# A new list of steps, up to the second batch, for an attention and gated-MLP kernel

## The chip, the cores and the metric

The kernel runs on one core of one Trainium2 chip. The metric is the device time of one execution in microseconds (us). The engines are TensorE (PE in the rows; PEld is its loading of weights), VectorE (DVE), ScalarE (ACT), GpSimd (POOL) and SyncE (SP), which issues the transfers (DMA).

## The reference

```python
def _attn_ref(q, k, v):            # 8 batches, 8 heads, 576 positions, head size 64
    scores = scale * np.matmul(q, k.transpose(0, 1, 3, 2))
    scores = np.where(mask, scores + bias[None], -1e9)   # 0 <= rel < 128; bias: -slope * |rel|
    scores = scores - np.max(scores, axis=-1, keepdims=True)
    attn = np.exp(scores)
    attn = attn / (np.sum(attn, axis=-1, keepdims=True) + 1e-09)
    return np.matmul(attn, v)

def _moe_ref(x, w_in, g_ln, w_sg, b_sg, w_out):          # x: attention out, 576 x 512 a batch
    h = gelu_tanh(x @ w_in)                              # 1024 wide
    u, v = h[..., :512], h[..., 512:]
    v_n = (v - mean(v)) / np.sqrt(var(v) + 1e-6) * g_ln
    v_s = np.einsum('ts,bsd->btd', w_sg, v_n) + b_sg[None, :, None]
    return x + (u * v_s) @ w_out
```

## The kernel before

The work is cut into 32 pairs of heads (four pairs to a batch) for the attention and into eight batches for the gated MLP. It is written as 2027 small steps, each a closure for one engine, with a name of a letter or two and numbers. The table of numbers is the string `ORDER`: the loop at the end takes the steps in that order, and each engine's instructions are tied into the order in which they are emitted. So an engine never goes past an instruction that waits, and the list alone decides what stands behind what. Buffers are handed out in list order too: a step that takes a buffer waits for the one that the list frees first.

The names that matter here, n being the pair (0 to 3 are batch 0, 4 to 7 batch 1):

- `q`n, `L`n: transfers of queries and keys, and of values. `i`k: transfer of one of 12 weight blocks (0 to 7 of w_in, 8 to 11 of w_out); `wl`c, `tl`, `bl`, `gb`: transfers of the spatial table w_sg, its bias and g_ln.
- `d`k (ScalarE, two instructions), `m`k, `b`k, `o`k (VectorE), `+`k (GpSimd), `H`k (ScalarE), `-`k (VectorE for odd k, GpSimd for even): a weight block is turned from 64 bits into a high and a low half. `wH`c, `w-`c: the same for w_sg.
- `a`n and `c`n (TensorE): scores; `*`n: both, from pair 5 on. `A B C G` (VectorE): bias and row minima of a quarter each; `e E f F j` (ScalarE): exponentials; `R` (VectorE): inverse sums; `s S r`: scaling (ScalarE or GpSimd); `t T z` (TensorE): transposes; `X Y` (VectorE): the masked halves that the product with the values needs; `P`, `p`: small copies on ScalarE for the first 64 rows; `V` (TensorE): product with the values; `x` (ScalarE) and `2`n (VectorE): its result to SBUF; `h` (ScalarE), `l` (GpSimd), `k`: its high and low halves, which the MLP multiplies.
- `w`tc and `v`bt (TensorE): the v half of the first MLP product, piece by piece for batch 0; `vg`: its gelu; `nv..`, `vn`: its norm; `u`bfi: the u half; `uc`: its copy out; `ug`: its gelu; `tt tj tg nt tn`: the same for the last 64 rows; `y`: the spatial product; `gm gh gl`: the gate; `O`, `oa`, `D`: the last product, its addition and its store.
- `W`i (TensorE): dummy products of a zero tile, 2 to 12 each, 51 in all, that compute nothing and need nothing but a PSUM bank. They are among the first steps in both lists.

A GpSimd step of the first stretch is one instruction; from the step `v33` on (`HALVED_FROM`) its large ones are cut in two. PSUM is three pools of two tiles (`ps_s`, `ps_a`, `ps_m`); v, u, y and O products take turns in `ps_m`. One ScalarE table holds the exponential, another the gelu, so a change from `e`-like steps to `vg`, `tg`, `ug` or back loads a table.

Of the kernel before, what the change touches and what calls it, by code (L numbers as in the profile page):

```python
# [21 lines left out]
def attention_gmlp(  # L22
# [1129 lines left out]
    ORDER = """
        q0 i2 d2 W8 W1 a0 c0 i1 A0 B0 m2 b2 o2 C0 e0 d1 E0 j0 f0 +2 G0 m1 F0 q1 a1 c1 b1 R0 A1 o1 B1 C1 wl2 i3 q3 i0
        L0 H2 wH2 W0 G1 s0 -2 S0 +1 w-2 t0 j1 d3 e1 r0 F1 E1 f1 X0 T0 W7 W2 W3 z0 W6 W11 P0 d0 Y0 m3 V0 b3 R1 o3 m0 b0
        o0 r1 z1 i5 wl3 p0 s1 +0 a3 A3 B3 W4 t1 W5 W10 c3 X1 C3 G3 wH3 d5 x0 e3 H0 f3 E3 20 S1 +3 w-3 -0 q2 L1 i6 i4
        L2 i7 h0 H1 F3 j3 P1 d6 T1 a2 Y1 A2 B2 l0 V1 R3 m5 s3 b5 -1 m6 o5 b6 o6 d4 x1 m4 21 +6 S3 t3 W9 X3 p1 r3 d7 h1
        j2 E2 e2 m7 c2 C2 G2 w00 z3 T3 w20 w30 f2 F2 P3 +5 l1 Y3 b7 R2 b4 o4 o7 s2 S2 +4 +7 L3 q5 V3 x3 23 i9 wl1 p3
        wH1 d9 r2 H5 q4 L4 i10 gb tl w10 t2 X2 T2 w11 z2 w01 Y2 H3 P2 h3 H7 V2 x2 p2 H4 l3 m9 b9 -3 -5 22 -7 w31 w21
        *5 A5 B5 h2 H6 e5 l2 w02 w32 v00 E5 vg00 v03 w12 v01 w22 v02 o9 C5 G5 nv00b nv00c -6 -4 +9 nv00p tH d10 k3 H9
        nv00h vg01 k2 -9 vn00 m10 b10 o10 vg03 f5 +10 u000 u001 nv30b nv30c nv10b nv30p H10 uc00 j5 nv30h F5 vn03 R5  # L1160
        nv10c -10 u030 a4 A4 u031 B4 vg02 k0 k1 e4 nv20b s5 r5 S5 nv10p w-1 t- nv20p t5 z5 c4 u020 X5 T5 C4 G4 Y5
        nv20c j4 uc03 E4 nv10h tt0 f4 P5 F4 nv20h i11 L5 q6 i8 bl q7 wl0 V5 u021 vn01 R4 vn02 tj0 d8 p5 x5 tg0 wH0 s4
        r4 S4 w-0 t4 25 X4 nt0b nt0p u010 z4 T4 u011 Y4 nt0c P4 uc02 d11 bH V4 nt0h p4 x4 uc01 ug0 b- tn0 m11 m8 24
        b11 o11 b8 y000 y001 *7 +11 gm00 A7 o8 +8 B7 C7 j7 e7 H11 -11 Us0 y020 y021 y030 G7 gm02 Us1 E7 H8 -8 gh00 f7
        h4 gh02 F7 Us2 *6 y010 Us3 R7 A6 B6 C6 s7 t7 S7 T7 y031 E6 gl02 r7 gl00 G6 X7 f6 e6 j6 F6 z7 y011 h5 L7 L6 q8
        q9 Y7 R6 gm03 gm01 P7 V7 gh03 gh01 p7 Uh0 s6 r6 S6 gl01 t6 T6 X6 x7 27 Y6 Oa0 gl03 z6 O00 P6 V6 Us4 oa00 h7
        Uh1 x6 p6 l7 l4 l5 26 Ul0 Ul1 O01 *8 A8 B8 C8 Us5 G8 h6 k5 f8 j8 e8 l6 u100 u101 k6 k7 E8 *9 Us6 F8 oa01 Us7
        A9 R8 B9 k4 Uh2 j9 uc10 u130 s8 r8 S8 u131 t8 u110 C9 uc13 E9 e9 f9 T8 tt1 X8 Ul2 G9 F9 R9 Y8 q10 Ud0 L9 D01
        Ud1 q11 L8 Ud2 D00 z8 u111 s9 r9 S9 tj1 Us8 uc11 P8 t9 V8 u120 tg1 x8 X9 28 Us9 nt1b T9 u121 Y9 nt1c O03 nt1p
        z9 Uh3 nt1h uc12 P9 Ul3 ks0 ks1 ks2 V9 p9 x9 p8 oa03 ks3 29 ks4 tn1 kh0 kh1 kl0 O02 ks5 *10 A10 B10 C10 G10  # L1170
        j10 e10 E10 f10 F10 oa02 kl1 v10 *11 v11 A11 R10 vg10 vg11 B11 nv01b nv01c C11 nv11b r10 s10 nv01p S10 nv11p
        z10 t10 ug1 v12 nv11c X10 v13 T10 P10 nv11h vn11 nv01h vn10 vg12 nv21b G11 vg13 nv31b Y10 nv21c nv31c ks6
        nv21p h9 l9 nv31p ya100 ya110 ya101 ya111 f11 e11 nv21h nv31h j11 kd0 q12 q13 L10 L11 D03 kd1 D02 V10 vn12 kh2
        F11 E11 vn13 y100 y101 y110 y111 ks7 kl2 gm10 ks8 ks9 R11 kh3 gm11 kl3 y120 y121 s11 t11 y130 gh11 gl11 y131
        x10 210 gm12 gt11 p10 h8 gh15 X11 gm13 O11 S11 gl15 r11 gt12 T11 z11 O15 h10 gh12 gh16 gh13 P11 Y11 oa11 gl12
        V11 x11 p11 gl16 gt13 O16 211 gh17 oa15 oa16 gt14 *13 gl13 O13 gl17 ut25 oa13 O17 A13 oa17 O12 B13 oa12 h11
        gh14 gl14 l8 O14 C13 oa14 G13 l10 l11 E13 k10 uh25 k9 k11 k8 v20 v21 vg20 ul25 vg21 j13 ut26 ut27 nv02b nv02c
        nv02p nv02h nv12b nv12p nv12c nv12h vn20 vn21 *12 tt2 U21 kd2 lu21 lu22 q14 lu20 L12 D11 D10 q15 L13 tj2 U25
        uh27 f13 uh26 e13 ue21 A12 B12 ut24 ul27 ul26 U26 F13 ue25 U23 uh24 E12 ue26 U27 C12 ue23 G12 R13 e12 f12 j12
        F12 U22 ue27 R12 ul24 U24 ue22 r12 s12 z12 t12 S12 tg2 nt2b nt2p s13 X12 nt2c ue24 v22 T12 Y12 v23 vg22 nv22b  # L1180
        P12 nt2h tn2 vg23 V12 p12 x12 nv32b nv32c 212 nv22c nv22p nv32p S13 h12 l12 r13 ug2 nv22h nv32h ya200 ya210
        *14 A14 B14 vn22 ya201 t13 ya211 z13 vn23 y200 y201 X13 gm20 C14 y210 y211 y220 T13 gm21 G14 E14 P13 f14 gh21
        j14 F14 e14 Y13 gl21 y221 *15 y230 R14 A15 gt21 B15 gm22 C15 r14 s14 S14 y231 gh25 f15 gm23 gl25 gt23 gt22 z14
        t14 V13 E15 gh23 P14 p13 x13 gh27 O21 gh22 j15 X14 213 lo21 q16 lo22 D13 q17 D12 lo20 L14 L15 T14 O25 G15 Y14
        gh26 V14 p14 F15 x14 e15 gl23 gl27 gl22 oa21 gl26 O26 oa25 O23 ut35 gt24 214 R15 oa26 oa23 *16 A16 B16 C16 O27
        s15 S15 r15 z15 t15 h14 k12 gh24 h13 E16 P15 j16 l13 gl24 l14 G16 oa27 X15 k13 e16 uh35 F16 f16 O22 T15 Y15
        O24 *17 R16 oa22 oa24 A17 B17 V15 s16 r16 S16 x15 p15 215 h15 ul35 l15 C17 f17 e17 t16 X16 T16 G17 ut37 Y16
        L16 q19 lu32 D21 lu30 D23 L17 q18 lu31 D20 v30 z16 k15 k14 j17 P16 F17 E17 tt3 tj3 *18 V16 R17 ut36 tg3 vg30
        nt3b nt3c nt3p uh37 x16 ul37 nt3h v31 216 nv03b tn3 U31 uh36 vg31 ue31 U35 A18 B18 nv13b ut34 ul36 U36 r17 s17
        t17 z17 ue35 uh34 ue36 C18 nv13c U33 ue33 X17 S17 nv03p nv13p ul34 U37 U32 ue37 T17 U34 nv13h P17 j18 E18 f18  # L1190
        vn31 ue32 G18 nv03c Y17 nv03h ue34 p16 F18 e18 vn30 v33 D22 R18 *19 vg33 V17 x17 ug3 A19 s18 B19 C19 nv33b 217
# [81 lines left out]
```

## Time and profile before

| | |
|---|---|
| median of 3 runs | 581.13 us (581.12 to 581.57) |
| the profiled execution | 581.97 us, of which the span of instructions is 580.3 us |
| TensorE, busy share of the span | 97% |
| VectorE | 82% |
| ScalarE | 66% |
| GpSimd | 53% |

Times in the rows count from the start of the span. A busy share is a mean over stretches that have different limits; matmuls overlap in the records, so a busy TensorE is one without pauses, not one at its peak. In a row, the bracket gives the idle time just before the instruction and what ended it; xN is the number of instructions that the row merges.

### The profile page before, as it was taken

To read this page: it belongs to the slowest core of one execution; us is meant where nothing else is said; L and a number is where in the kernel's file an instruction comes from. 1 tells how busy PE (TensorE), PEld (TensorE's weight loads), DVE (VectorE), ACT (ScalarE), POOL (GpSimd) and SP (SyncE) were. 2 spreads that over 40 slices of the span, in tenths; PEclk is the share of its full clock that TensorE was granted. 3 is DMA by queue.
4 is the path that set the end of the run, shared out by engine and by line. 5 is a ranking of instruction groups with operands and counts; after the bars stand their busy time and mean duration, and the time that the engine had idled before them with its cause. 6 is when DMAs were issued, how large, how long until landed. Compare 5 with 4: busy or idle time off the path is not lost.

```text
span 580.3 us, 14668 instructions
## 1 busy us (share of the span) xinstructions
...
## 2 busy tenths in 40 slices
...
GB/s 299 212 224 107 127 102 83 7 272 33 210 37 64 215 37 98 144 180 141 60 184 38 105 236 167 48 101 153 143 121 64 211 4 196 3 32 98 171 1 82
DMA packets 43562, 69.79 MB, mean 120 GB/s; under 512 B 3554, under 2 KB 31202, under 8 KB 43492
## 3 DMA queue, kind: packets, MB, share of 16 engines
...
HBM read 56.27 MB, written 12.58 MB: 119 GB/s over the span
## 4 chain that ended last, share of the span: by engine, by line
PE 86%; DVE 4%; DMA 3%; ACT 3%; POOL 2%; issue 1%; SPq 0%; DVEq 0%; POOLq 0%
PE ps_m L1061 13%; PE ps_m L609 12%; PE ps_m L907 12%; PE ps_m L611 11%; PE ps_m L610 11%; PE ps_a L350 4%; PE ps_a L281 4%; PE ps_s L387 3%; PE ps_m L387 3%; PE ps_s L281 3%; DMA wst<-w_sgT 2%; DMA qk<-qkT 1%; PE ps_m L943 1%; PE ps_m L942 1%; DVE e L298 1%
## 5 line engine op out<-in xcount | busy, mean ns | idle before, releaser
L337 POOL TENSOR_TENSOR e<-e,rr 128x256 f32<-128x256 f32 (+2 forms) x116 | 80.3, 715 | 95.1 <-DVE rr L326 90.5
L314 ACT ACTIVATE e<-e,stats 128x128 f32<-128x128 f32 (+1 forms) x288 | 110.6, 386 | 19.4 <-DVE stats L298 18.9
L227 POOL TENSOR_TENSOR region<-u,region 128x288 fp32r<-128x288 f32 (+1 forms) x78 | 77.6, 1014 | 44.8 <-ACT region L1008 16.2
L359 DVE TENSOR_TENSOR px<-ps_a,m_both 128x1024 f32<-128x1024 f32 x64 | 77.4, 1215 | 6.2 <-PE ps_a L350 4.9
L609 PE MATMUL ps_m<-ws,region 128*128 128x288 f32 x256 | 78.3, 306 | 0.0
L611 PE MATMUL ps_m<-ws,region 128*128 128x288 f32 x256 | 75.7, 296 | 0.0
L610 PE MATMUL ps_m<-ws,region 128*128 128x288 f32 x256 | 75.6, 295 | 0.0
L732 POOL TENSOR_TENSOR rs<-rs,mhalf 128x1 f32<-128x1 f32 (+1 forms) x40 | 30.6, 766 | 58.3 <-DVE rs L729 54.6
L221 POOL TENSOR_TENSOR xs<-xf,xs 128x288 fp32r<-128x288 f32 (+1 forms) x48 | 51.1, 1086 | 14.5 <-ACT xs L404 14.5
L314 ACT ACTIVATION_READ_ACCUMULATOR e<-e,stats 128x1 f32 x288 | 54.3, 189 | 0.0
L1008 ACT ACTIVATE region<-u 128x576 fp32r<-128x576 f32 x35 | 23.6, 684 | 43.4 <-PE ps_m L610 17.4
L609 PEld LDWEIGHTS ps_m<-ws,region 128*128 128x128 f32 x256 | 48.3, 189 | 1.5 <-issue 1.1
L610 PEld LDWEIGHTS ps_m<-ws,region 128*128 128x128 f32 x256 | 48.2, 188 | 0.1
L611 PEld LDWEIGHTS ps_m<-ws,region 128*128 128x128 f32 x256 | 48.1, 188 | 0.1
L609 PE MATMUL ps_m<-wi,xs 128*128 128x512 f32 x112 | 46.7, 417 | 0.9 <-ACT vg L788 0.9
L1068 DVE TENSOR_TENSOR xf<-ps_m,xf 128x576 f32<-128x576 f32 x48 | 35.7, 750 | 10.9 <-PE ps_m L1061 10.1
L611 PE MATMUL ps_m<-wi,xs 128*128 128x512 f32 x112 | 44.3, 395 | 0.0
L610 PE MATMUL ps_m<-wi,xs 128*128 128x512 f32 x112 | 44.2, 395 | 0.0
L948 DVE TENSOR_TENSOR u<-ps_m,u 128x576 f32<-128x576 f32 x32 | 24.0, 750 | 19.7 <-PE ps_m L943 12.6
L350 PE MATMUL ps_a<-ident,e 128*128 128x128 f32 x256 | 38.0, 276 | 0.2
L298 DVE CUSTOM_DVE_ANT_0 e<-ps_s,bias 128x128 f32<-128x128 f32 (+1 forms) x140 | 34.9, 286 | 2.6
L1061 PE MATMUL ps_m<-region,sum 128*128 128x288 f32 x252 | 36.5, 298 | 0.0
(213 smaller groups left out, 1606.2 us busy)
## 6 DMA issues: line engine op xcount, KB each, us to landing
...
```

Source lines behind the costliest of these rows:

```text
L221: (engine or nc.gpsimd).tensor_tensor(out[:, cs], a[:, cs], b[:, cs], op)
L227: nc.gpsimd.tensor_tensor(out[:, fs], a[:, fs], b[:, fs], ALU.subtract)
L298: nc.vector.tensor_tensor_reduce(out=dst, in0=src, in1=bs, scale=-1.0 / math.sqrt(D), scalar=3e38, op0=ALU.add, op1=ALU.min, accum_out=acc)
L314: nc.scalar.activation(x, x, AF.Exp, bias=self.nm[0:n, i:i + 1], scale=-1.0, accum_out=self.sm[0:n, i:i + 1])
L337: nc.gpsimd.tensor_tensor(x[:, z:z + step, :], y[:, z:z + step, :], self.rr[0:n, i + z:i + z + min(k, step)].rearrange("p (m o) -> p m o", ...
L350: burst([lambda t=t: nc.tensor.transpose(cv[:, t // 2, t % 2], self.pr[j][:, t, :].rearrange("p (h c) -> p h c", h=2), ident[:, j * R:j * ...
L359: nc.vector.tensor_tensor(xv, cv, mv, ALU.mult)
L609: nc.tensor.matmul(dst, ah, bh, start=(first and i == 0), stop=False)
L610: nc.tensor.matmul(dst, ah, bl, start=False, stop=False)
L611: nc.tensor.matmul(dst, al, bh, start=False, stop=(last and i == n - 1))
L907: nc.tensor.matmul(dst, left(n, g, c)[:, ms], right(n, h, c), start=first and c == 0 and k == 0, stop=c == 1 and k == 2, skip_group_check= ...
L1061: nc.tensor.matmul(dst, p, q, start=first and f == 0 and k == 0, stop=f == 1 and k == 2, skip_group_check=True)
```

## The change

The list is a new one from its start to the step `V10` (631 steps, some 162 us into the execution); what follows is as before. The same steps are in it, with the same instructions and sizes; only their order differs, and with it which buffer of a pool a step gets. Among the moves: fourteen dummy products instead of eight ahead of the first scores, the weight blocks in the order 2, 0, 1, 4, 3 instead of 2, 1, 3, 0, 5, the tables w_sg 2 and 3 much later, and the scores of pair 4 ahead of most u products.

```diff
-        q0 i2 d2 W8 W1 a0 c0 i1 A0 B0 m2 b2 o2 C0 e0 d1 E0 j0 f0 +2 G0 m1 F0 q1 a1 c1 b1 R0 A1 o1 B1 C1 wl2 i3 q3 i0
...
+        q0 i2 q1 W3 W2 W4 W10 a0 c0 W9 W1 W5 a1 A0 B0 d2 C0 m2 G0 b2 o2 A1 i0 +2 e0 E0 f0 F0 j0 d0 B1 R0 j1 s0 m0 b0
...
```

The first place is ScalarE up to the copy P0 (`p_0`), which pair 0's product V0 needs. `e` and `stats` with 126 are pair 0's, with 128 pair 1's; L193 and L195 are a d step, L314 exponentials, L332 scalings. From pair 1's first exponentials (j1 before, E1 now) on, before:

```order
L314 ACTIVATE e_1_124,stats_128<-e_1_124,stats_128 128x64
L193 ACTIVATE wst<-wst 128x512
L195 ACTIVATE tmp<-wst 128x512
L314 ACTIVATE e,stats_128<-e,stats_128 128x128 x2
L332 ACTIVATE e_0_122<-e_0_122,rr 128x64
L314 ACTIVATE e,stats_128<-e,stats_128 128x128 x6
L366 COPY p_0_119<-ps_a 128x128
L193 ACTIVATE wst<-wst 128x512
L195 ACTIVATE tmp<-wst 128x512
```

and now:

```order
L314 ACTIVATE e,stats_128<-e,stats_128 128x128 x2
L193 ACTIVATE wst<-wst 128x512
L195 ACTIVATE tmp<-wst 128x512
L314 ACTIVATE e,stats_128<-e,stats_128 128x128 x6
L193 ACTIVATE wst<-wst 128x512
L195 ACTIVATE tmp<-wst 128x512
L332 ACTIVATE e_1_124<-e_1_124,rr 128x64
L332 ACTIVATE e_0_122<-e_0_122,rr 128x64
L332 ACTIVATE e<-e,rr 128x128 x4
L193 ACTIVATE wst<-wst 128x512
L195 ACTIVATE tmp<-wst 128x512
L366 COPY p_0_119<-ps_a 128x128
```

Before, the copy stood behind the weights 2, 1 and 3; now the weights 0, 1, 4 and 3 (beside 2) and the scaling of pair 1 stand ahead of it.

The second place is VectorE ahead of the two masked halves of pair 2 (L359, X2 and Y2), from the inverse sums R2 (L325, L326) on; L399 is the step 23. Before:

```order
L325 TENSOR_SCALAR rr<-stats_130 128x9
L326 RECIPROCAL rr<-rr 128x9
L199 TENSOR_SCALAR tmp<-tmp 128x512
L201 SCALAR_TENSOR_TENSOR tmp<-wst,tmp 128x512 x2
L399 TENSOR_TENSOR xf_134<-ps_s,xf_134 128x512
L359 TENSOR_TENSOR px<-ps_a,m_both 128x4x256 x2
L197 TENSOR_SCALAR tmp<-tmp 128x512
L199 TENSOR_SCALAR tmp<-tmp 128x512
```

and now:

```order
L325 TENSOR_SCALAR rr<-stats_130 128x9
L326 RECIPROCAL rr<-rr 128x9
L197 TENSOR_SCALAR tmp<-tmp 128x512
L211 TENSOR_TENSOR wi<-tmp,wi 128x512
L199 TENSOR_SCALAR tmp<-tmp 128x512
L201 SCALAR_TENSOR_TENSOR tmp<-wst,tmp 128x512
L399 TENSOR_TENSOR xf_134<-ps_s,xf_134 128x512
L359 TENSOR_TENSOR px<-ps_a,m_both 128x4x256 x2
```

Before, b4, o4 and o7 (L199, L201) stood between, and m9 and b9 behind X2 and Y2; now m9, the subtraction -1 (L211), b9 and o9 stand ahead of them.

The third place is ScalarE's first gelus of v (L788) with the table loads, the exponentials of pairs 5 and 4 (L314), the norms' high halves (L740) and the copy uc00 (L842). Before:

```order
L788 ACTIVATE vg<-ps_m 128x512
L410 CAST xs<-xs 128x64
L788 ACTIVATE vg<-ps_m 128x512
L314 ACT_TABLE_LOAD
L314 ACTIVATE e,stats_130<-e,stats_130 128x128 x2
L206 ACTIVATE wo<-tmp 128x512
L842 COPY u<-ps_m 128x576
L314 ACTIVATE e_1_124,stats_130<-e_1_124,stats_130 128x64
L740 ACTIVATE region<-vg,rs 128x4x128
L314 ACTIVATE e,stats_130<-e,stats_130 128x128 x2
L1239 ACT_TABLE_LOAD
L1239 ACTIVATE warm<-mhalf 128x1
```

and now:

```order
L1239 ACT_TABLE_LOAD
L1239 ACTIVATE warm<-mhalf 128x1
L788 ACTIVATE vg<-ps_m 128x512 x2
L314 ACT_TABLE_LOAD
L314 ACTIVATE e,stats_130<-e,stats_130 128x128 x6
L314 ACTIVATE e_1_124,stats_130<-e_1_124,stats_130 128x64
L314 ACTIVATE e_0_122,stats_128<-e_0_122,stats_128 128x64
L740 ACTIVATE region<-vg,rs 128x4x128 x2
L842 COPY u<-ps_m 128x576
L1239 ACT_TABLE_LOAD
L1239 ACTIVATE warm<-mhalf 128x1
L788 ACTIVATE vg<-ps_m 128x512 x2
```

Before, vg00 stood alone a few rows ahead and vg01 and vg03 came one by one; now vg00 and vg01 stand together, then the exponentials, uc00, and vg02 and vg03 together.

## Rows read from the trace of the kernel before

**Rows 1.** Busy time by stretch: PE, PEld, DVE, ACT, POOL; clock, DMA share, GB/s

```profile
0.00:64.00 64.00, 52.45 (x504) 41.00 (x505) 56.40 (x197) 56.49 (x175) 37.70 (x43) 0.95 0.66 213
64.00:165.00 101.00, 100.95 (x1071) 91.44 (x1070) 90.70 (x271) 74.47 (x215) 44.54 (x45) 1.00 0.32 106
165.00:580.00 415.00, 410.11 (x3925) 381.86 (x3924) 329.76 (x870) 250.45 (x678) 226.85 (x278) 1.00 0.34 110
```

**Rows 2.** Waits of TensorE, 44 to 66 us: total, times, longest

```profile
PE ps_m L609 <- ACT vg L788: 1.3, 2, 0.9
PE ps_m L609 <- ACT u L842: 1.1, 1, 1.1
```

**Rows 3.** Timeline of TensorE: start, length, what, idle time before it

```profile
1.32 1.33 PE L1141 MATMUL ps_m<-spare 128*128 128x288 f32 x4 [1.32 <-DVE spare L91]
...
4.66 1.56 PE L281 MATMUL ps_s<-qk 64*64 64x128 f32 x20 [1.06 <-DMA qk<-qkT]
...
29.49 3.43 PE L387 MATMUL ps_s<-px,vt 64*64 64x128 f32 x36 [1.72 <-issue]
...
32.50 0.48 PE L391 MATMUL ps_a<-p,vt 64*64 64x64 f32 x4
...
34.91 1.69 PE L281 MATMUL ps_s<-qk 64*64 64x192 f32 x16
...
46.67 1.58 PE L387 MATMUL ps_s<-px,vt 64*64 64x128 f32 x36
...
63.34 0.40 PE L609 MATMUL ps_m<-xs,wi 128*128 128x288 f32 x1 [1.11 <-ACT u L842]
...
68.27 0.88 PE L281 MATMUL ps_s<-qk 64*64 64x192 f32 x16
```

**Rows 4.** Timeline of VectorE

```profile
13.14 1.17 DVE L201 SCALAR_TENSOR_TENSOR tmp<-wst,tmp 128x512 int32<-128x512 int32 x1
...
19.88 0.63 DVE L201 SCALAR_TENSOR_TENSOR tmp<-wst,tmp 128x512 int32<-128x512 int32 x1
...
25.16 0.29 DVE L305 COPY_PREDICATED ps_s<-sel,ps_s 128x128 f32<-128x128 uint8 x1 [0.23 <-PE ps_s L281]
...
41.04 2.05 DVE L201 SCALAR_TENSOR_TENSOR tmp<-wst,tmp 128x512 int32<-128x512 int32 x2
...
43.61 2.34 DVE L359 TENSOR_TENSOR px<-ps_a,m_both 128x1024 f32<-128x1024 f32 x2
...
45.87 0.41 DVE L197 TENSOR_SCALAR tmp<-tmp 128x512 f32<-128x512 f32 x1
...
46.80 0.69 DVE L211 TENSOR_TENSOR wi<-tmp,wi 128x512 fp32r<-128x512 f32 x1
```

**Rows 5.** Waits of VectorE, 24 to 64 us

```profile
DVE rr L325 <- ACT e L314: 0.5, 1, 0.5
```

**Rows 6.** Timeline of ScalarE

```profile
6.03 0.67 ACT L193 ACTIVATE wst<-wst 128x512 int32<-128x512 uint32 x1 [1.81 <-DMA wst<-w_in]
...
17.32 0.39 ACT L314 ACTIVATE e<-e,stats 128x128 f32<-128x128 f32 x1
...
18.86 0.25 ACT L366 COPY p<-ps_a 128x128 f32<-128x128 f32 x1
...
20.17 0.33 ACT L332 ACTIVATE e<-e,rr 128x64 f32<-128x64 f32 x1
...
20.72 1.28 ACT L332 ACTIVATE e<-e,rr 128x128 f32<-128x128 f32 x4
...
30.63 0.24 ACT L366 COPY p<-ps_a 128x128 f32<-128x128 f32 x1
...
46.60 0.24 ACT L366 COPY p<-ps_a 128x128 f32<-128x128 f32 x1
```

**Rows 7.** Groups of GpSimd by line, 9 to 64 us: the tables

```profile
L221 POOL TENSOR_TENSOR ws<-wst,ws 128x576 fp32r<-128x576 f32 x2 | 2.9, 1428 | 0.0
```

**Rows 8.** Busy time by stretch, columns as in rows 1

```profile
29.20:35.90 6.70, 6.29 (x56) 4.70 (x60) 5.94 (x21) 6.70 (x21) 2.62 (x2) 0.50 0.49 155
```

More of the change, by code (lines that the diff above doesn't have):

```diff
@@ L1152, in attention_gmlp @@
     ORDER = """
-        q0 i2 d2 W8 W1 a0 c0 i1 A0 B0 m2 b2 o2 C0 e0 d1 E0 j0 f0 +2 G0 m1 F0 q1 a1 c1 b1 R0 A1 o1 B1 C1 wl2 i3 q3 i0
[L1154 to L1172, printed above, removed]
@@ new lines, in attention_gmlp @@
+        o0 +0 S0 i1 q3 L0 i4 i3 L1 i6 c1 t0 W8 T0 C1 G1 X0 E1 d1 f1 e1 F1 d4 m1 b1 o1 +1 Y0 R1 m4 b4 o4 r1 r0 s1 W0 z1
+        a3 W11 z0 +4 A3 B3 d3 P0 V0 H4 p0 H2 x0 e3 d6 m3 b3 c3 t1 W7 C3 G3 X1 S1 o3 m6 -4 -2 20 F3 f3 H0 E3 +3 -0 q2
+        i7 gb L3 i5 q4 i9 P1 h0 j3 d7 T1 a2 W6 Y1 A2 B2 d5 l0 R3 m7 b6 b7 m5 o6 b5 o5 o7 V1 s3 E2 x1 e2 21 t3 w20 X3
+        S3 +7 +5 p1 d9 j2 r3 h1 c2 w30 z3 T3 w00 C2 l1 f2 P3 G2 F2 H1 Y3 R2 m9 -1 b9 o9 s2 S2 +6 +9 L2 wl0 q5 i10 wl1
+        wl3 V3 x3 23 r2 p3 k0 H3 wH0 H7 d10 w21 t2 X2 w01 T2 Y2 z2 w31 h3 P2 H6 V2 x2 H9 p2 w10 l3 m10 -3 b10 22 o10
```

52 lines of the change are left out of this document (33 added, 19 removed).

## The prediction

> **What bounds the kernel now.** I read the busy time by stretch first [rows 1]. From 64 to 165 us TensorE is busy for 100.95 of 101.00 us, so there its own work sets the time, and whatever it is ahead at 64 us stays ahead to the end. Before 64 us it is busy for 52.45 us, of which some is dummy products (W) that compute nothing; VectorE (56.40) and ScalarE (56.49) are the full ones there, GpSimd (37.70) is not. So the list of steps is worth what it does to the moment at which TensorE gets its work without a pause. The waits of TensorE between 44 and 66 us [rows 2] say where that moment is lost last: 1.3 us in two waits for a gelu of v (vg) and 1.1 us for a copy of u (uc00), together 2.4. The last ends at 63.34 us, where u030 starts [rows 3]. No later wait of TensorE is seen up to 165 us.
>
> **The measure.** I compare the start of u030 in both lists, and count what TensorE has done by then. Before: V2 starts at 46.67, u030 at 63.34, so 16.67 us, of which 2.4 are those waits. The new list has the same products between V2 and u030 (two of the w steps change places across V2 with two others) and two more, the score groups a4 and c4, which before run behind u030 (c4 at 68.27) [rows 3].
>
> **The three waits of 54 to 63 us.** In the old list v02, v12 and the rest alternate between the two banks while ScalarE has one vg to do for either, with e, d and H steps between. In the new one v00 and v01 are both ahead of vg00 and vg01, which ScalarE does back to back, and a4, v02 and c4 stand between u000, u001 and u030. While ScalarE does the exponentials of pair 5 and uc00, TensorE has 0.88 + 0.88 us of scores (c4 [rows 3]; a4 has the same kind of group) and v02. I therefore take all 2.4 us as gone. ScalarE does not get easier: vg02 and vg03 now come behind uc00, but u030 takes the bank that uc00 frees, as before, and u020, which needs theirs, comes two u steps later.
>
> **What is late instead: V2.** V2 needs the last masked half of pair 2 (Y2, VectorE). Before, X2 and Y2 run from 43.61 for 2.34 us, to 45.95 [rows 4]. The changes ahead of Y2 on VectorE, one by one:
> 1. The start. Fourteen dummy products stand ahead of a0 instead of eight. Eight run from 1.32 to 3.60 (a0 at 4.66 less its wait of 1.06 [rows 3]), 0.285 each; fourteen end at 5.3. The transfer of q0 hid the first eight, and hides the next ones only up to 4.66. VectorE's first minima are 0.5 late, an estimate.
> 2. More work ahead of it. m9, b9 and o9 ran behind Y2 and now run ahead of X2: 0.93 for m9 and b9 (45.87 to 46.80) and 0.63 for an unhindered o step (19.88) [rows 4], 1.55 us.
> 3. Its waits. Before, 0.23 us for c3 (25.16 [rows 4]) and 0.5 for the exponentials of pair 3 [rows 5]: 0.7 in all. After: c3 stands behind V0, as before, and V0 cannot end before ScalarE has copied p0 (P0). Ahead of P0 ScalarE has 5 d steps of 1.16 (from 18.86 + 0.15 to 20.17), 16 exponentials of 0.39, two short ones of some 0.35, two scalings s of 1.28 and two r of 0.3 [rows 6]: 5.8 + 6.2 + 0.7 + 2.5 + 0.6 = 15.8 us from 6.03, and some 1.6 us in four waits for VectorE (e0 behind A0, F0 behind G0, s0 behind R0, r1 behind R1; an estimate). That puts P0 at 23.5 where it was at 18.86. A V step starts without its P (V1 starts at 29.49 [rows 3], its P1 at 30.63 [rows 6]; only its last small products, 32.50, need it), so V0 ends at 24.0 and c3 at 24.9. VectorE gets to C3 at 24.5: before it was ready at 24.93, it has m4, b4, o4 more (1.4), X1 and o3 less (1.17 and 0.63 [rows 4]), the start's 0.5 and one hindrance less (next point). So it waits 0.4 there. C2 follows c2, which follows t3 and so s3, which ScalarE does behind d7 and d5; I estimate 0.7 of wait. Together 1.1, 0.4 more than before.
> 4. Hindrances. The o step of weight 1 took 1.17 us at 13.14, and o4 and o7 together 2.05 at 41.04, against 0.63 at 19.88 [rows 4]: 0.54 + 0.79 = 1.33 us lost, I think to GpSimd, which reads the same kind of operands at those times. In the new list most o steps stand where GpSimd's next instruction is the sum (+) that waits for that very o; o9 and the subtraction -1 can meet the scaling S2 or the sum +6. I count two meetings of 0.45, 0.9 us, so 0.45 less than before.
> Sum: 0.5 + 1.55 + 0.4 - 0.45 = 2.0. Y2 ends at 47.95, and V2 starts 1.3 us later than at 46.67 (before, TensorE itself came 0.7 us after Y2; that slack is used up). P2 is no bound: at 46.60 before [rows 6], it gets d10 (1.16) and an h more ahead of it, and only V2's last products need it, 1.3 us behind its start.
>
> **The sum.** 2.4 us of waits gone less 1.3 us of lateness: TensorE is 1.1 us ahead. Behind u030 each engine has the steps that it had, less what was done earlier, and TensorE is full; VectorE's 90.70 busy of 101 us [rows 1] would cover 1.1 us. On SP's queue the keys q1 go ahead of the weights i1, and the tables wl2 and wl3 leave their places among the first eleven transfers for places behind i10 and L5; DMA has a share of 0.66 up to 64 us [rows 1], and I find no step of the sum that comes up before its transfer can have landed, so I cost that at nothing (a late one would hold the d step behind it, and ScalarE with it, for as long as it is late). The tables' subtractions w-2 and w-3 on GpSimd, 1.43 us each [rows 7], now come later, w-3 with the first norms and w-2 just ahead of y000. GpSimd is busy for 44.54 of the 101 us from 64 [rows 1], so that is hidden too; without that cover it would be 2.9 us ahead of y000. The profiled execution (581.97 us, span 580.3) becomes 580.9; it stands 0.84 over the median of the runs, 581.13, so the forecast is 581.13 - 1.1 = 580.0.
>
> **A rule that speaks against it.** The Trainium skill, page "SBUF — State Buffer", section "Who interferes with whom", says that VectorE with two operands in SBUF and a GpSimd instruction that reads SBUF exclude each other for a whole instruction, and that the first to be issued wins. The o step has two such operands; 1.17 against 0.63 agrees. By that rule the new list's price is one GpSimd instruction's rest for each meeting, and the second rival follows.
>
> **Rivals.**
> - *V2 is not late.* If the waits for c3 and c2 and the two meetings do not occur (0.4 + 0.7 + 0.9), Y2 is at 45.95, V2 at 46.67, and all 2.4 us are gain: 578.7. For it: each is an estimate of mine. Against: VectorE has 1.55 us more to do ahead of Y2 in any case.
> - *VectorE is hindered as often as before or more.* Three more meetings of 0.54 (1.17 less 0.63) are 1.6 us; V2 is then 2.9 late and the waits save 2.4: 0.5 slower, 581.6. For it: VectorE has no gap to absorb them. Against: GpSimd has a smaller share of that stretch.
> - *The clock (slower).* TensorE's granted clock was 0.50, that is 1.2 GHz, from 29.2 to 35.9 us [rows 8], after a pause of 1.72 us ahead of V1 [rows 3]. There V1 took 3.43 us instead of V2's 1.58, and c2 1.69 instead of c4's 0.88. In the new list TensorE pauses earlier: from c1 (some 11 us) it waits for s0 at 14.6, then for S0 at 17.2 and for r1 at 20.7, with only 4 and 12 dummy products between. If the clock is at 1.2 GHz at 22 us, a3, V0 and c3 take 0.6 + 1.85 + 0.81 us more, and as C3 is already the wait of VectorE there, Y2 and V2 are 3.2 us later, less some 0.4 of the wait counted for c2, which then shrinks: 581.13 - 1.1 + 2.8 = 582.8. It decides when c3 ends later than 27 us. Against it: the twelve products of W0 fill 3.4 us of these pauses at 0.285 each. The Trainium skill, page "TensorE: Matmul & The Clock Gate", section "What's actually happening", has the low clock as the state of rest that activity lifts; by it a pause is paid twice.
>
> **Chances.** Forecast 0.37, V2 not late 0.25, hindered 0.19, clock 0.19. The forecast's 1.1 us is about 0.2% (1.16 us), which is what a measurement here can tell from no change, so it counts half to either side. Faster by more than 0.2%: 0.25 + 0.19 = 0.44; within: 0.18 + 0.17 = 0.35; slower: 0.19 and a little of the hindered case, 0.21. The range takes in the first rival with 0.4 of room for a start that is not late (578.3) and the clock (582.8); the forecast's own range is 579.2 to 580.9.
>
> **What the profile after would show.** Right: no wait of TensorE for vg or u between 54 and 64 us; V2 at about 48; u030 at about 63.9 with a4 and c4 done (that is 1.1 ahead); P0 at 23 to 24; C3 waiting under 1 us; the first minima at 6.8. Wrong: a granted clock of 0.50 between 15 and 30 us and V0 above 3 us (third rival); o steps at 1.1 us and more in numbers (second); V2 at 46.7 (first); or a wait of TensorE behind 64 us, at y000 for the late tables or at t7, which would mean that what was saved is given back.

## The result: 5.4 us slower, and where it shows in the profile after

The changed kernel takes 586.74 us (median of 6, 586.21 to 588.36) against 581.35 (6, 581.06 to 581.68): a ratio of 1.0096 (95% interval 1.0082 to 1.011). The forecast was 580.0, its range 578.3 to 582.8. The profiled execution took 586.21, its span 584.5, 4.2 more than before's. Busy time by stretch after, as in [rows 1]:

```profile
0.00:64.00 64.00, 50.91 (x515) 40.02 (x516) 57.89 (x200) 55.28 (x178) 35.15 (x42) 0.92 0.58 190
64.00:165.00 101.00, 98.62 (x1004) 88.49 (x1003) 92.45 (x262) 71.62 (x194) 48.38 (x46) 1.00 0.38 120
```

In the first stretch VectorE is busy for 1.49 us more (57.89 against 56.40) and TensorE for 1.54 less. In the second TensorE is no longer full: 2.38 us of 101 are pauses, where it had 0.05. So there are two losses. TensorE's waits, from 44 to 70 us (as [rows 2]) and from 70 to 165 us, where before had none:

```profile
PE ps_a L363 <- DVE px L359: 1.6, 1, 1.6
PE ps_m L609 <- ACT u L842: 1.5, 1, 1.5
PE ps_m L610 <- DVE wi L211: 0.2, 1, 0.2
```

```profile
PE ps_a L281 <- ACT xf L369: 0.4, 1, 0.4
PE ps_m L610 <- POOL xs L221: 0.2, 1, 0.2
PE ps_s L281 <- DVE xf L399: 0.2, 1, 0.2
```

The two waits for vg are gone, as forecast, but the one for uc00 (u, L842) is longer than before's 1.1. TensorE's timeline, as in [rows 3], at a0, V2, c4 and u030:

```profile
4.98 1.56 PE L281 MATMUL ps_s<-qk 64*64 64x128 f32 x20
...
49.73 1.58 PE L387 MATMUL ps_s<-px,vt 64*64 64x128 f32 x36
...
64.74 0.88 PE L281 MATMUL ps_s<-qk 64*64 64x192 f32 x16
67.13 0.40 PE L609 MATMUL ps_m<-xs,wi 128*128 128x288 f32 x1 [1.51 <-ACT u L842]
```

V2 is 3.06 us late (46.67 before; the forecast allowed 1.3), u030 3.79. As a4 and c4 are then done, 1.77 of it is left, and this stays the same from tt0 to `*7`. VectorE ahead of V2 (m3, b3 and the first row of C3; b6 with b7; -1 and b9; X2 with Y2), and GpSimd beside it (-4; S3; S2 and +6):

```profile
24.21 0.70 DVE L197 TENSOR_SCALAR tmp<-tmp 128x512 f32<-128x512 f32 x1
24.95 1.40 DVE L199 TENSOR_SCALAR tmp<-tmp 128x512 int32<-128x512 int32 x1
26.27 0.28 DVE L305 COPY_PREDICATED ps_s<-sel,ps_s 128x128 f32<-128x128 uint8 x1
...
34.15 1.61 DVE L199 TENSOR_SCALAR tmp<-tmp 128x512 int32<-128x512 int32 x2
...
43.24 1.56 DVE L211 TENSOR_TENSOR wi<-tmp,wi 128x512 fp32r<-128x512 f32 x1
44.73 1.52 DVE L199 TENSOR_SCALAR tmp<-tmp 128x512 int32<-128x512 int32 x1
...
47.50 2.34 DVE L359 TENSOR_TENSOR px<-ps_a,m_both 128x1024 f32<-128x1024 f32 x2
```

```profile
24.58 1.48 POOL L221 TENSOR_TENSOR wi<-tmp,wi 128x512 fp32r<-128x512 f32 x1
...
34.09 1.04 POOL L337 TENSOR_TENSOR e<-e,rr 128x512 f32<-128x512 f32 x1 [0.42 <-DVE rr L326]
...
43.22 1.04 POOL L337 TENSOR_TENSOR e<-e,rr 128x512 f32<-128x512 f32 x1 [0.80 <-DVE rr L326]
44.21 1.75 POOL L221 TENSOR_TENSOR tmp<-tmp,wst 128x512 int32<-128x512 int32 x1
```

A b step (L199) takes 0.41 when GpSimd is still (36.61 in the same timeline), b3 1.40: -4 begins at 24.58 and ends at 26.06, and b3 ends 0.29 behind that. m3 waits likewise for S1 (23.58 to 24.63), b6 (34.15, with b7) for S3, -1 for S2, b9 for +6. The five rows are 4.0 us over their unhindered lengths (0.28, 0.99, 0.79, 0.88 and 1.11; a subtraction takes 0.68, an m step 0.42). Counted from the end of the step before, and with R1 and R3 (0.26 and 0.23), it is 4.7 us, which the expectations below put at 4.9; before has 1.8 by the same count, so the new list has 2.9 more.

The second loss, at `*8` and u100, by engine, from the trace after: TensorE, VectorE (Us3 and Us4; 26), ScalarE (Uh1, p6, x6), GpSimd (l7 and l5; l6):

```profile
115.73 0.70 PE L281 MATMUL ps_a<-qk 64*64 64x192 f32 x14 [0.42 <-ACT xf L369]
116.94 0.87 PE L281 MATMUL ps_s<-qk 64*64 64x192 f32 x12 [0.18 <-DVE xf L399]
119.16 0.40 PE L610 MATMUL ps_m<-xs,wi 128*128 128x288 f32 x1 [0.22 <-POOL xs L221]
```

```profile
111.26 3.65 DVE L651 TENSOR_TENSOR sums<-sums,wi 128x512 f32<-128x512 f32 x2
116.19 0.69 DVE L399 TENSOR_TENSOR xf<-ps_s,xf 128x512 f32<-128x512 f32 x1 [1.28 <-ACT xf L396]
```

```profile
114.94 0.63 ACT L658 ACTIVATE sum<-sums 128x512 fp32r<-128x512 f32 x1 [4.13 <-DVE sums L651]
115.48 0.19 ACT L369 COPY xf<-ps_a 128x64 f32<-128x64 f32 x1
```

```profile
110.89 3.47 POOL L221 TENSOR_TENSOR xs<-xf,xs 128x576 fp32r<-128x576 f32 x2 [1.88 <-ACT xs L404]
117.67 1.43 POOL L221 TENSOR_TENSOR xs<-xf,xs 128x576 fp32r<-128x576 f32 x1 [3.31 <-ACT xs L404]
```

Us3 and Us4 take 3.65 us together beside l7 and l5. On ScalarE Uh1 waits for them, with p6 and x6 queued behind it, which free the banks that `*8` takes; on VectorE 26 waits for x6, h6 and l6 follow, and u100 needs l6. Before, `*8` ran without a wait; now 1.89 us are lost from its start to u101.

### The profile page after: what moved, and what is told of

Read it like the earlier page. It is cut to its first block, busy times and chain, and to the rows that moved or that the text cites. A ratio compares the mean times of both kernels' runs of the same rounds, so it can differ in the third digit from the quotient of the medians.

```text
span 584.5 us, 14675 instructions
## 1 busy us (share of the span) xinstructions
PE 563.8 (96%) x5495; PEld 514.1 (88%) x5495; DVE 484.6 (83%) x1336; ACT 381.9 (65%) x1066; POOL 310.6 (53%) x365
## 4 chain that ended last, share of the span: by engine, by line
PE 87%; DVE 8%; DMA 1%; issue 1%; ACT 1%; POOL 1%; SPq 0%; DVEq 0%; ACTq 0%
PE ps_m L1061 13%; PE ps_m L609 12%; PE ps_m L907 12%; PE ps_m L610 11%; PE ps_m L611 11%; PE ps_a L350 4%; PE ps_a L281 4%; PE ps_m L387 3%; PE ps_s L387 3%; PE ps_s L281 3%; DVE e L298 2%; PE ps_m L943 1%; PE ps_m L942 1%; DVE px L359 1%; PE ps_m L798 1%
## 5 line engine op out<-in xcount | busy, mean ns | idle before, releaser
L337 POOL TENSOR_TENSOR e<-e,rr 128x256 f32<-128x256 f32 (+2 forms) x116 | 81.8, 728 | 96.5 <-DVE rr L326 90.1
L314 ACT ACTIVATE e<-e,stats 128x128 f32<-128x128 f32 (+1 forms) x288 | 110.7, 387 | 17.4 <-DVE stats L298 16.9
L359 DVE TENSOR_TENSOR px<-ps_a,m_both 128x1024 f32<-128x1024 f32 x64 | 77.3, 1216 | 5.0 <-PE ps_a L350 4.7
L314 ACT ACTIVATION_READ_ACCUMULATOR e<-e,stats 128x1 f32 x288 | 54.4, 189 | 0.0
L350 PE MATMUL ps_a<-ident,e 128*128 128x128 f32 x256 | 39.3, 281 | 7.1 <-ACT e L332 3.0
L350 PEld LDWEIGHTS ps_a<-ident,e 128*128 128x128 f32 x256 | 30.9, 143 | 10.6 <-issue 6.5
```

Of the source, the lines that this page charges most:

```text
L314: nc.scalar.activation(x, x, AF.Exp, bias=self.nm[0:n, i:i + 1], scale=-1.0, accum_out=self.sm[0:n, i:i + 1])
L337: nc.gpsimd.tensor_tensor(x[:, z:z + step, :], y[:, z:z + step, :], self.rr[0:n, i + z:i + z + min(k, step)].rearrange("p (m o) -> p m o", ...
L350: burst([lambda t=t: nc.tensor.transpose(cv[:, t // 2, t % 2], self.pr[j][:, t, :].rearrange("p (h c) -> p h c", h=2), ident[:, j * R:j * ...
L359: nc.vector.tensor_tensor(xv, cv, mv, ALU.mult)
```

## The experiments

The table gives, for each kernel, its median, the ratio to before with its interval, and how far TensorE stands behind (+) before's profiled execution at the start of five steps in its own. That execution is itself late at V2, by 1.1 to 1.5 us against three other kernels with the old beginning. Its trace shows why: ScalarE waits twice for a table (wH3 and wH1, for the transfers wl3 and wl1), and then z2 on TensorE, which stands ahead of V2, waits for the scaling r2, which stands behind wH1 on ScalarE. That wait is the longest in the window of [rows 2], and is not among its lines.

```profile
23.39 0.69 ACT L572 ACTIVATE ws<-wst 128x576 fp32r<-128x576 f32 x1 [1.39 <-DMA wst<-w_sgT]
...
43.59 0.69 ACT L572 ACTIVATE ws<-wst 128x576 fp32r<-128x576 f32 x1 [0.92 <-DMA wst<-w_sgT]
```

```profile
45.70 0.33 PE L363 MATMUL ps_a<-ident,e 128*128 128x128 f32 x1 [1.56 <-ACT e L332]
```

In the kernel "old, then new" there is no such wait for a table, Y2 ends 0.65 us earlier, z2 waits 0.8 us for VectorE, V2 is 1.42 and `*7` 0.88 earlier. Against that execution the new list is 4.48 late at V2 and 2.65 at `*7`.

| kernel | us | ratio | V2 | `*7` | `*8` | u101 | `*10` |
|---|---|---|---|---|---|---|---|
| the new list | 586.74 | 1.0096 (1.0082 to 1.011) | +3.06 | +1.77 | +1.89 | +3.78 | +3.97 |
| new, then old | 585.10 | 1.0064 (1.0049 to 1.0079) | +3.06 | +1.78 | +2.43 | +2.43 | +2.43 |
| old, then new | 584.00 | 1.0045 (1.003 to 1.006) | -1.42 | -0.88 | -0.49 | +1.40 | +1.72 |
| short sums, new | 582.79 | 1.0018 (1.0008 to 1.0027) | +1.12 | -1.44 | -1.73 | +0.15 | +0.15 |
| short sums, old | 581.97 | 1.0008 (0.9998 to 1.0018) | -0.36 | -0.58 | -0.65 | -0.65 | -0.65 |
| two later | 584.00 | 1.0044 (1.0031 to 1.0057) | +1.05 | -0.47 | -0.35 | +1.53 | +1.74 |
| halved, new | 585.04 | 1.0054 (1.0029 to 1.0079) | +3.20 | +0.96 | +0.67 | +0.82 | +1.96 |
| halved, old | 583.61 | 1.0037 (1.0026 to 1.0048) | -1.06 | +0.18 | +0.30 | +0.30 | +0.30 |
| uc00 ahead | 586.93 | 1.0087 (1.0067 to 1.0106) | +4.23 | +2.81 | +2.91 | +4.80 | +5.01 |
| Uh1 behind x6 | 586.18 | 1.0084 (1.0067 to 1.0101) | +3.06 | +1.76 | +1.89 | +2.83 | +2.99 |
| 26 first | 587.29 | 1.0101 (1.0086 to 1.0116) | +4.21 | +2.91 | +3.01 | +3.00 | +5.02 |
| sums ahead | 585.60 | 1.008 (1.0051 to 1.0108) | +3.79 | +2.49 | +2.60 | +2.60 | +3.80 |
| W0 early | 589.33 | 1.0121 (1.0088 to 1.0154) | +6.20 | +4.92 | +5.04 | +6.93 | +7.40 |
| all three | 583.41 | 1.0041 (1.0028 to 1.0054) | +0.73 | -0.80 | -0.69 | -0.69 | +0.69 |
| more dummies | 584.40 | 1.0051 (1.0037 to 1.0065) | +1.86 | +0.36 | +0.06 | +0.06 | +1.84 |
| two later, then old | 582.54 | 1.0024 (1.0014 to 1.0034) | +1.82 | +0.31 | +0.96 | +0.96 | +0.96 |
| old with a4 | 580.91 | 0.9995 (0.9986 to 1.0004) | -1.50 | -1.33 | -1.34 | -1.34 | -1.34 |

### Which half of the list

New, then old: the new list up to `*7`, the remaining steps in the old order.

```diff
-        ... *7 A7 gm00 B7 +11 +8 y020 y021 y030 e7 ...
+        ... *7 +11 gm00 A7 +8 B7 C7 j7 e7 ...
```

> The new list up to the score step *7, from there the remaining steps in the order of the old list. Theory (two separate losses: one up to u030 because VectorE's steps are stretched by GpSimd instructions beside them, 1.8 us on TensorE by *7; another at *8 and u100, because on ScalarE the step Uh1 waits for Us4 and holds p6, x6 and h6 behind it, 1.9 us): only the first remains, about 2 to 2.5 us over before, 583.3 to 583.9. Rival 1 (the loss at *8 follows from being late at *7): all of it remains, about 586.5. Rival 2 (what is lost early is made up later, and the late part is the whole loss): about 581.4.

Old, then new: the reverse.

```diff
-        ... *7 +11 gm00 A7 o8 +8 B7 ...
+        ... *7 L7 o8 A7 gm00 B7 +11 +8 ...
```

> The old list up to *7, then the remaining steps in the order of the new list. Theory: TensorE is in time up to *7, and the second loss remains, 2 to 3 us over before, 583.4 to 584.4, with a wait in *8 for p6 (ACT xf) as in the new kernel. Rival 1 (the loss at *8 follows from being late at *7): about 581.4 and no wait in *8. Rival 2 (the late part is the whole loss): about 586.5.

Both lists' parts cost something: 3.9 us for the new beginning and 2.8 for the new rest, each against 581.25 in the same comparison. The second is as expected; the first is 1.2 us over its range, in part because the 1.8 us were counted from before's profiled execution, which lies 0.7 over that median. The sum, 6.6, is over the 5.4 of both, in part because the old order has a loss of its own behind the new beginning: 0.65 between `*7` and `*8`. The loss of 1.89 from `*8` to u101 is the same in the new list (1.89), behind the old beginning (1.89) and with short sums (1.88), so it does not come from being late.

### What made V2 late

The GpSimd instructions of the first part cut short, in the new and the old list:

```diff
-        by_halves(ALU.add, fi, fi, ri)
+        by_halves(ALU.add, fi, fi, ri, short=True)
...
+        if short and not halved:
+            out, n = out[:, 0:SHORT], SHORT
...
-                step = 2 if m == T and halved else m
-                for z in range(0, m, step):
+                step = 2 if m == T and halved else 1 if m == T else m
+                for z in range(0, m if halved or m != T else 1, step):
```

> The new list with GpSimd's instructions of the first 350 us cut short: the sums + and the differences - of the weight blocks and of w_sg go over 64 of their columns only (448 to 512 are left out, the low halves there are zero, set once ahead of the first step), and its scalings S over one of four blocks. So part of the computation is left out; the steps, their order and VectorE's, ScalarE's and TensorE's instructions are those of the new list. Theory (VectorE's steps beside GpSimd's instructions are stretched, 4.9 us up to Y2 in the new list against 1.8 in the old one, and that is what makes V2 late): the stretch up to Y2 falls under 1 us, Y2 ends at 46 to 46.5 instead of 49.9, and the time is 583 to 584, that is 2.7 to 3.7 under the new list; what is left over is the second loss, behind *7. Rival (the order itself, the work that now stands ahead of Y2 and its waits): Y2 not before 48.5, 585.5 or more.

> The old list with the same edit (the same part of the computation is left out). Theory: it has 1.8 us of stretch up to Y2 to lose and waits of 2.4 us behind V2 that do not depend on it, so 580 to 581, and the new list with the edit stands 0.5 to 1 us behind it in Y2 (three steps more ahead of it, a later start) and 2.5 to 3.5 us in all, against 5.4 without the edit. Rival: it stands as far behind as without the edit, 5 us.

The same steps of VectorE with short sums, new list (-1, b9, and X2 with Y2):

```profile
42.93 0.92 DVE L219 TENSOR_TENSOR wi<-tmp,wi 128x512 fp32r<-128x512 f32 x1
43.77 0.54 DVE L207 TENSOR_SCALAR tmp<-tmp 128x512 int32<-128x512 int32 x1
...
45.56 2.35 DVE L369 TENSOR_TENSOR px<-ps_a,m_both 128x1024 f32<-128x1024 f32 x2
```

Setting the low halves to zero lets the first minima start at 8.07 us in both kernels, later by 1.45 us in the new list and by 1.77 in the old, so they are compared with each other; the new list's later start of 0.32 us is then not in the comparison, and GpSimd's results come sooner in both. The stretch up to Y2 is 1.1 and 0.3 us. V2 is then 1.48 later in the new list, not 3.06 or more, and at `*7` the new list is 0.86 us ahead (-1.44 against -0.58). Behind that it loses 1.88 at `*8`, and ends 0.82 slower by the medians, where 2.5 to 3.5 were expected; in Y2 it stands 1.67 behind (47.91 against 46.24), where 0.5 to 1 were expected. So without the meetings the first part would have been a gain: 0.86 us, or some 0.5 with the later start, an estimate.

Two GpSimd steps moved, with no work left out:

```diff
-        ... S1 o3 m6 -4 -2 ... s2 S2 +6 +9 L2 ... w10 l3 m10 ...
+        ... S1 o3 m6 -2 ... s2 S2 +9 +6 L2 ... w10 l3 -4 m10 ...
```

> The new list with two GpSimd steps moved to places behind +9 and l3, where their results are still early enough: the sum +6 (so that it no longer runs beside b9) and the difference -4 (so that it no longer runs beside b3). VectorE's, ScalarE's and TensorE's orders stay. Theory: b9 and b3 take 0.42 us again, Y2 and V2 come 1.5 to 2.3 us earlier, and as the waits at u030 may then take some of it, the time is 584.6 to 585.8. Rival (other meetings or waits take the place of these two): Y2 less than 0.8 us earlier, 586.3 or more.

VectorE at b3 and from b9 on, and TensorE's waits from 44 to 70 us:

```profile
24.95 0.43 DVE L199 TENSOR_SCALAR tmp<-tmp 128x512 int32<-128x512 int32 x1
...
43.82 0.41 DVE L199 TENSOR_SCALAR tmp<-tmp 128x512 int32<-128x512 int32 x1
...
45.48 2.35 DVE L359 TENSOR_TENSOR px<-ps_a,m_both 128x1024 f32<-128x1024 f32 x2
```

```profile
PE ps_m L611 <- POOL xs L221: 0.7, 1, 0.7
PE ps_a L363 <- DVE px L359: 0.5, 1, 0.5
PE ps_m L609 <- ACT u L842: 0.2, 1, 0.2
```

Both steps have their length again, Y2 ends 2.0 us earlier (47.83 against 49.84), and the wait for uc00 falls from 1.51 to 0.2. At `*7` TensorE is 2.24 ahead of the new list. The time fell by 2.7, more than expected: these two meetings are half of the loss.

Halves, which test that it is whole instructions that exclude each other:

```diff
-    HALVED_FROM = "v33"
+    HALVED_FROM = "q0"
```

> The new list with every large GpSimd instruction cut in two from the start, as the kernel does from v33 on. Theory (a VectorE step that comes second is held until the whole GpSimd instruction ends): no step is stretched by more than 0.7 us (b3, b6, -1 and b9 now 0.9 to 1.2), the stretch up to Y2 falls from 4.9 to 2.5 to 3.5, and the time to 584.7 to 585.7. Rival (both engines run on at a lower rate beside each other, whatever the length of an instruction): the same stretch, 4.5 or more, and 586.5 or more, with a little for the additional instructions.

> The old list with every large GpSimd instruction cut in two from the start. Theory (whole instructions exclude each other): its stretch up to Y2 (1.8 us, o1 0.54, o4 0.90, m7 0.38) falls by half at most, and 0.1 us comes to each cut instruction: 580.5 to 581.5, so the new list with the same edit (585.0) stays 3.5 to 4.5 behind. Rival (halves help any list as much as they helped the new one, 1.7 us): 579.6.

b3, -1, b9 and o9 in the new list with halves:

```profile
24.59 0.84 DVE L199 TENSOR_SCALAR tmp<-tmp 128x512 int32<-128x512 int32 x1
...
44.07 1.13 DVE L211 TENSOR_TENSOR wi<-tmp,wi 128x512 fp32r<-128x512 f32 x1
45.13 0.83 DVE L199 TENSOR_SCALAR tmp<-tmp 128x512 int32<-128x512 int32 x1
46.00 1.12 DVE L201 SCALAR_TENSOR_TENSOR tmp<-wst,tmp 128x512 int32<-128x512 int32 x1
```

A meeting costs 0.4 to 0.45 instead of 0.9 to 1.1, which the rival does not give. But b7 and o9 now have one too, so that the stretch up to Y2 only falls to some 4 us (2.5 to 3.5 were expected), and Y3 waits 1.22 us for a transposition, so V2 did not come earlier; the gain, 1.7, comes at u030 and `*8`. The old list with halves missed both expectations: level with before up to `*10` (+0.30), it then loses 1.4 us up to `*18`; why was not followed up.

The wait for uc00 by itself:

```diff
-        ... j4 R5 nv10h vn01 nv00h uc00 ...
+        ... j4 uc00 R5 nv10h vn01 nv00h ...
```

> The new list with the copy uc00 moved on ScalarE from behind nv10h and nv00h to ahead of them. Theory (u030 waits 1.51 us for uc00 because it stands behind nv10h, which waits 1.17 us for VectorE): the wait goes, u030 starts 1.4 us earlier and the time is 585.0 to 585.5, 1.2 to 1.7 under the new list, if y000 does not wait for nv10h and nv00h, which end 0.6 us later at most. Rival (what is saved there is lost again before *7): 586.2 to 587.2.

The rival held. From V2 to `*7` TensorE makes up 1.42 us, in the new list 1.29, so only 0.13 of the 1.5 was kept.

### The second loss

```diff
-        ... oa00 Us2 Us3 Us4 h7 Uh1 p6 x6 26 Uh0 h6 ...
+        ... oa00 Us2 Us3 Us4 h7 p6 x6 Uh1 26 Uh0 h6 ...
```

> The new list with one step moved: Uh1 behind p6 and x6, so that ScalarE copies pair 6's product out before it waits for Us4. On VectorE the step 26 still stands behind Us2, Us3 and Us4. Theory: the wait in *8 for p6 (0.4 us) goes, 26 comes 1.3 us earlier (at the end of Us4, about 115.0 instead of 116.25), and u100 gets l6 1.3 us earlier: 1.0 to 1.4 us under the new kernel. Rival (GpSimd's own order l7 l5 l6 sets u100): no change.

```diff
+        ... oa00 h7 p6 x6 26 h6 Us2 Us3 Us4 Uh1 Uh0 ...
```

> The new list with 26 and h6 ahead of Us2, Us3, Us4, Uh1 and Uh0 (VectorE and ScalarE). Theory: 26 at about 112.3, h6 at 113, l6 directly behind l5 at 114.4 to 116, so that the waits of *8 and u100 go almost entirely: 1.7 to 2.2 us under the new kernel, about 0.6 under the kernel in which only Uh1 is moved. Rival (GpSimd's l7 and l5, stretched beside Us3 and Us4, set it): no better than with Uh1 moved alone.

```diff
+        ... Y6 27 Us2 Us3 Us4 gl01 Oa0 gl03 ... oa00 h7 Uh1 p6 x6 26 ...
```

> The new list with VectorE's three sums Us2, Us3, Us4 ahead of oa00 (where VectorE is idle for 0.99 us and GpSimd too, from 108.7 to 110.6) instead of behind it, beside l7 and l5. Theory of the second loss (*8 and u100 come 1.9 us late because Us3 and Us4 are stretched to 1.8 us each ahead of 26, and Uh1, p6, x6, h6, l6 wait for them): all of it goes, *8 takes 1.53 us, *9 stands where *7 stood against before (1.8 late), and the time is 584.3 to 585.2. Rival (as when 26 was put ahead of the three: the time is lost again at tt1 and z8): 586.2 or more.

With Uh1 behind x6 the loss from `*8` to u101 is 0.94 instead of 1.89 (the wait for l6 is left), and the time is 0.56 under the new list's, about half of what was expected. With 26 first, or with the three sums ahead of oa00, it is gone: in the kernel with the sums ahead VectorE has Us3 and Us4 in 1.42 us instead of 3.65, and 26 at 113.05 against 116.19, and then nothing to do for 2.80 us until `*8`:

```profile
110.31 1.42 DVE L651 TENSOR_TENSOR sums<-sums,wi 128x512 f32<-128x512 f32 x2
...
113.05 0.69 DVE L399 TENSOR_TENSOR xf<-ps_s,xf 128x512 f32<-128x512 f32 x1 [0.66 <-ACT xf L396]
116.55 0.30 DVE L305 COPY_PREDICATED ps_a<-sel,ps_a 128x128 f32<-128x128 uint8 x1 [2.80 <-PE ps_a L281]
```

But 2.0 and 1.2 us are lost again between u101 and `*10`: z8 waits 0.6 us for VectorE in both, tt1 0.9 in the first; the rest was not traced. Both times missed their expectations (587.29 and 585.60). The cause is shown, the repair is not complete. In these two V2 also came 0.7 to 1.1 us later than in the new list's profile; whether that holds for their medians is not shown. That the stretch of the sums is part of the cause shows in the new list with halves, too: with the order unchanged, Us3 and Us4 take 1.18 and 1.19 us there, and `*8` to u101 loses 0.15.

### Together, and the start

```diff
-        ... 26 Uh0 h6 l7 ... *9 Ul1 oa01 Ul0 Us5 ...
+        ... 26 Uh0 h6 Ul1 Ul0 l7 ... *9 oa01 Us5 ...
```

> The new list with +6 and -4 later (as in the run with these two), the sums Us2, Us3, Us4 ahead of oa00 (as in the run with those) and the sums Ul1, Ul0 behind 26 and h6, in VectorE's idle time of 2.80 us ahead of A8, instead of behind G8. Theory (three named places make up the loss: b3 and b9 beside GpSimd, 26 behind three sums, and X8 and Y8 late for z8 because Ul1 and Ul0 stand ahead of them): TensorE is 0.5 us ahead of before at *7, and keeps all but 0.5 of it to z9; the time is 580.7 to 581.7, level with before. Rival (a further cause): 582.5 or more.

> The new list with +6 and -4 later up to *7, and from there the old list's order of the steps that are left. Theory (the first part is then 0.5 us ahead at *7, and the old order loses nothing at *8 and z8; but in the run with the new list first and the old one behind, 0.7 us was lost between *6 and T7): 581.0 to 582.0. Rival (the old order behind *7 suits the new beginning badly): 582.8 or more.

All three repairs bring TensorE to 0.69 ahead of before at u101, and 1.38 us are lost up to `*10`, of which 0.7 are waits at tt1 and z8 (0.2 and 0.5); at 583.41 the rival held: a further cause is left. The mended beginning with the old rest (a plain joining of lists at `*7`) loses 0.65 ahead of `*8` and nothing behind it, and is the better of the two, yet at 582.54, between theory and rival, it is 1.3 us slower than before: in its profiled execution the new beginning came to c3 0.8 later than with the two steps moved alone.

The last point is a spread of the start between executions. W0 moved from behind s1 to ahead of t0, and eight more products added there:

```diff
-        ... i6 c1 t0 W8 ... r0 s1 W0 z1 ...
+        ... i6 c1 W0 t0 W8 ... r0 s1 z1 ...
```

> The new list with the twelve dummy products W0 ahead of t0, in TensorE's pause of 3.0 us at 10.7, instead of behind s1. Theory of the first stretch (the granted clock of 0.5 at 14 to 20 us makes a3 late in some runs, and A3 on VectorE waits for it up to 1.07 us; this is the spread of 1 us between runs of the new list): the clock is 1.0 there or a pause later, and the time 585.8 to 586.5, with runs 0.3 us apart. Rival (the dummy products now hold t0 and with it X0 back): 586.7 or more.

> The same as the kernel with all three, with eight more dummy products in TensorE's pause of 3.0 us at 10.7, ahead of t0 (W0 and all others stay). Theory (the granted clock of 0.5 at 14 to 20 us makes a3 late in some runs): the clock does not fall there, c3 ends by 25, and the time is 0.2 to 0.8 under that kernel's, its runs closer to each other. Rival (the products hold t0, or the clock falls all the same): the same or slower.

With W0 ahead of t0 TensorE pauses for 2.75 us up to 21.2; the clock, and V0 (1.52 for the same row in the new list):

```profile
20.00:26.00 6.00, 4.80 (x50) 4.00 (x54) 4.61 (x20) 3.73 (x11) 3.66 (x4) 0.50 0.58 184
```

```profile
24.09 2.77 PE L387 MATMUL ps_m<-px,vt 64*64 64x128 f32 x34
```

This is what the forecast's third rival describes: a granted clock of 0.50 (1.2 GHz) at 22 us, V0 over 3 us with its rest, c3 ended at 27.9, and V2 3.1 us later than in the new list; the time is 589.33. In the new list as it is, the clock was 0.51 from 14 to 20 us, but 0.92 from 20 to 26, and V0 took its usual time. In five other kernels with the new beginning A3 waited 0.8 to 1.07 us for a3; eight more dummy products did not remove that (1.07, and 584.40 us), and what decides it is open.

### One part alone, in the old list

```diff
-        ... nv10c -10 u030 a4 A4 u031 ...
+        ... nv10c -10 a4 u030 A4 u031 ...
```

> One part of the change alone: the old list with the score group a4 ahead of u030, where TensorE waits 1.11 us for uc00, instead of behind it; nothing else is moved. Theory (the forecast's saving was right in itself: work that is ready fills that wait, and TensorE stays ahead by what was filled, 0.88 us): 580.3 to 580.7, faster than before by 0.1 to 0.2%. Rival (what is saved there is given back at the next wait, as it was when uc00 was moved in the new list): 581.0 or more.

TensorE's waits from 44 to 66 us:

```profile
PE ps_a L363 <- DVE px L359: 0.8, 1, 0.8
PE ps_m L609 <- ACT vg L788: 0.7, 1, 0.7
PE ps_m L611 <- POOL xs L221: 0.7, 1, 0.7
PE ps_m L609 <- ACT u L842: 0.3, 1, 0.3
```

The wait for uc00 falls from 1.1 [rows 2] to 0.3. By the position at `*7`, against the other kernel with the whole old beginning (-0.88), 0.45 us are kept; the medians differ by 0.29 (580.91 against 581.20), between the theory and the rival, and a measurement here can't tell that from no change. It is the fastest kernel of all, but not shown to be faster than before.

## Why the prediction was wrong

- **The saving.** Right in kind: the waits for vg went, and a4 and c4 ran ahead of u030. "I therefore take all 2.4 us as gone" failed for the copy: the last exponentials and nv10h stand ahead of uc00 on ScalarE, and nv10h waited 1.17 us for VectorE's nv10c. With VectorE 2.0 us earlier (two later) that wait is 0.2, so it followed from the next point.
- **V2: the start, the work, the waits.** Forecast 0.5, 1.55 and 0.4. a0 came 0.32 late (4.98 against 4.66); VectorE's waits up to Y2 did not grow but shrank by 0.5 (0.25 us for a3, none for c3 or the exponentials), as VectorE was itself later than its data. The three more steps took 1.35, counted from the end of the step before. P0 came at 23.63 (23.5 forecast), c3 ended at 25.2 (24.9).
- **V2: the hindrances. This is the step that failed.** I counted "two meetings of 0.45", 0.45 us less than before. There were seven, three of them small (0.2 to 0.35): 2.9 us more than before (4.7 against 1.8). The count looked at o steps and the subtraction -1 alone, since before's largest cases were o steps. What was hit were the b steps of 3, 6 and 9, an m step, -1 and two inverse sums; and b3, b6, -1 and b9, beside -4, S3, S2 and +6, lost 0.8 to 1.1 us each, most of a GpSimd instruction, not 0.45. Cutting GpSimd short and moving two of its steps both show it. Before's trace held the sign: an m step (m7, behind X3) took 0.74 us beside S3. The Trainium skill's section quoted there ("SBUF — State Buffer", "Who interferes with whom") names tensor_scalar, the one-operand form of m and b, too, in its two-port modes, and this trace agrees: 1.40 against 0.41 us. So the second rival was the case. It gave 2.9 us for V2, and 3.06 were measured, but that is luck, errors that cancel: its hindrances were 1.15 us over before's, not 2.9, and its waits and its start were too large. What it lacked are the wait for uc00 and `*8`.
- **"Behind u030 each engine has the steps that it had ... and TensorE is full."** Wrong at `*8`: 1.88 or 1.89 us are lost in every kernel that has the new order there with whole GpSimd instructions. A busy share of VectorE (90.70 of 101 us) says nothing about which step stands behind which; the order of Us2 to Us4, Uh1, p6, x6 and 26 was in the lists and was not compared.
- **The execution it counts from.** "before, TensorE itself came 0.7 us after Y2": that slack was z2's wait for r2 behind the late tables, which "old, then new" does not have and the new list does not either. So the 0.84 us by which the profiled execution lies over the median are not common to both lists, as the last step of the sum has it: 0.88 of the 1.1 us that were forecast are what "old, then new" already has at `*7`. With all else as forecast the time would have been about 580.9, an estimate from 581.13, 1.1 and 0.88, which rests on one execution of each kernel.
- **The tables and the transfers** cost nothing in the new list, as forecast: no step on ScalarE waits for a table there, and TensorE's lag is 1.75 to 1.78 from tt0 to `*7`.
- **The clock** was a real rival, avoided by the place of W0's twelve products, as argued (W0 early: 589.33).
- The sum: V2 late by 3.06 and a wait of 1.51 instead of 1.3 and none make TensorE 1.77 late at `*7` instead of 1.1 ahead; 0.1 is lost ahead of `*8`, 1.89 behind its start, 0.2 up to `*10` and 0.3 behind it, 4.2 in all. The profiled execution of before lay 0.6 over its median and that of after 0.5 under, which is the rest of the 5.4.
